# Block-sparse attention and a feed-forward on one core: P buffers, the order of weight conversion, and where adds run

## The chip, the cores and the metric

One core of one Trainium2 chip. The metric is the device time of one execution in microseconds. The kernel before has a median of 794.09 us in three runs (792.69 to 794.2).

## What is computed

Four batches, 8 heads of 64, 768 positions. Scores are q·kT/8; blocks of 32 keys that the pattern doesn't allow (window, first and last block, three sampled blocks a row) are set to -1e9; softmax; times v. The result, 768 x 512 a batch, goes through a normalized feed-forward with a residual. In the reference, cut:

```
attn = exp(scores - max); attn = attn / (sum(attn) + 1e-9); x = attn @ v
xn = (x - mean(x)) / sqrt(var(x) + 1e-6) * g_ln
out = x + maximum(xn @ w_ch1, 0) @ w_ch2        # w_ch1 512 x 2048, w_ch2 2048 x 512
```

The weights arrive as 64-bit floats, everything else as 32-bit.

## The kernel before, in words

**Tiling.** A *unit* is one batch's chunk of 256 queries: 12 units, three a batch. A unit has four *segments*, one a pair of heads, 48 in all; a segment has four *slots* (128 queries of one head). Two slots, the two heads for the same queries, are scored together: pair k holds slots 2k and 2k+1. Every fp32 operand of TensorE is split into two fp16 halves, high and low, and a product is three matmuls (high·high, low·high, high·low), except in the early segments.

**A slot's way.** `scores` (L591) into a PSUM tile `ps` (two of them); `masked_max` (L600, VectorE) writes the biased, negated scores to a tile P and their extreme to `st`; `exponent` (L614, ScalarE) turns P into exponentials. In the first nine segments (EARLY) TensorE transposes P in fp32 (L629) into one of three PSUM banks and ScalarE copies it out to `pt` (L636), and `weighted` (L714) multiplies by v in fp32. In later segments `attention` makes P's fp16 halves, high on ScalarE (L675), low on VectorE (L679), into places `ph` and `pl`, two each or, from segment WIDEAT on, four; SP transposes them by DMA (L685, L688), and `weighted` (L718, L723) follows. When a unit's four segments are done, `layer_norm` runs through VectorE, ScalarE and TensorE down to `xh` (L859) and `xl` (L863), and `ffn` does W1 then W2 (all in `product`, L306): 384 matmuls of 256 columns a unit.

**Weights.** W1 has 8 chunks (1,i), W2 16 chunks (2,i) of half the size. `loads_w` loads a chunk (L497, L507), and makes fp32 out of the 64-bit words in three steps on VectorE (L518, L522, L526). A chunk in PORC has a short third step instead (L531) and an add on GpSimd (L536). Then comes a scaling on ScalarE (L554) if the chunk is in neither PORC nor LOWDVE, the high half on ScalarE (L560, L562) or, if it is in both HIDMA and PORC, by a DMA (L572), and the low half: on VectorE (L568) if it is in LOWDVE, else on GpSimd (L566). Chunks of W2 from the third on are loaded when all of W1 is converted, those from the eleventh on when the first ten of W2 are.

**What sets the order.** All engines run an order that is written at build time. `Plan` is a list scheduler with a cost and a latency for every task; each engine takes, of the tasks that could start now, the one of lowest rank. Ranks are counted in slots: W1AT and W2AT for the chunks, KAT, VAT and QAT for loads, MASKAT for the second half of the mask, which slot 16 needs. Feed-forward matmuls have the last rank and fill what is left. EASE is the spare time that the planner leaves before a task that waits for another engine: its first value for ranks under EASY on TensorE, its second beyond, its third for other engines beyond EASY. A task with `lock` isn't started by the planner while GpSimd or VectorE holds one. Where TensorE would idle before KEEP (ns), the planner puts fillers (L298). AVHOLD = n: from segment 12 on, the weighted sum of segment i isn't issued before pair 2i+n. CASTK: the high half of K is cast on ScalarE (L362) for the first so many of the 16 K, by a DMA on GpSimd's queue after that; KDVE and QDVE: how many low halves of K (L355) and q (L391) VectorE makes, GpSimd the others.

**P's memory.** P is one of four rotating tiles; a slot takes one at its masked maximum and gives it back when its transposes (early) or its low half (later) are done. The places for the fp16 halves are tiles of their own.

Of the kernel before, what the change touches and what calls it, by code (L numbers as in the profile page):

```python
# [176 lines left out]
def sparse_attention_moe(  # L177
# [32 lines left out]
    EASY, EASE = 44, (249, 2530, 951)  # L210
    PORC = ((2, 0), (2, 7), (1, 1), (2, 11), (2, 9), (1, 6), (2, 13), (2, 10), (1, 4), (2, 1), (2, 2))
# [26 lines left out]
    pp = ctx.enter_context(tc.tile_pool(name="pp", bufs=2))  # L238
# [11 lines left out]

    plan = Plan()
# [92 lines left out]
    def loads_k(b, pr, rank, before):  # L344
        idx = b * NPAIR + pr
        o = SimpleNamespace()

        def raw():
# [3 lines left out]
            nc.sync.dma_start(o.kr, ks[b, pr])  # L352
# [4 lines left out]
        o.raw = plan.add("SP", 580, raw, (before,), rank, 2000, load=1120, order="k",  # L357
# [12 lines left out]
    def loads_q(n, rank, before):  # L370
        u, pr = segs[n].u, segs[n].pr
        o = SimpleNamespace()

        def raw():
# [62 lines left out]
    def loads_v(b, pr, rank, before):  # L437

        o = SimpleNamespace(idx=b * NPAIR + pr, vr={}, raw=[])
        early = any(x.early for x in segs if (x.u.b, x.pr) == (b, pr))  # L440
# [11 lines left out]
        for j in range(2):  # L452
            def raw(j=j):
# [18 lines left out]
    def loads_w(kind, i, before, w1done, low_tail):  # L472

        o = SimpleNamespace()
        own = (kind, i)
        if kind == 1:
# [11 lines left out]
        def load():  # L488
# [18 lines left out]
            nc.sync.dma_start(o.raw.rearrange("p e t -> p (e t)"),  # L507
# [33 lines left out]
        ld = plan.add("SP", 580, load, after if kind == 1 or i >= 10 else after + tuple(  # L541
# [52 lines left out]
    def masked_max(s):  # L594
        s.p = pp.tile([P, S], F32, tag="p", name=f"p{s.i}", bufs=4)
# [21 lines left out]
    def attention_early(seg, pair, e_done):  # L617
        r = pair[0].i
        for s in pair:
            key = (seg.i, s.h % 2)  # L620
            x4 = x2 = None
            for part, (lo, hi) in enumerate(((0, 4), (4, KT))):
# [18 lines left out]
                take = (("pt", key),) if s.t == 0 and part == 0 else ()  # L641
# [498 lines left out]
```

## Time and profile before

| | |
|---|---|
| median of three runs | 794.09 us |
| the profiled execution, its own time | 793.85 us |
| its span in the trace | 792.1 us |
| TensorE busy | 777.9 us |
| VectorE busy | 616.1 us |
| ScalarE busy | 507.2 us |
| GpSimd busy | 123.5 us |

The span runs from the first to the last instruction in the trace; the own time has in addition what lies around it. Durations in rows are of that one execution. In rows, PE is TensorE's matmuls, PEld its weight loads, DVE VectorE, ACT ScalarE, POOL GpSimd, SP the queue that issues most DMAs. Matmuls are pipelined and overlap in the rows: the distance from start to start is their cost. A wait for several semaphores is put down to the one that came last.

### The profile page before, as it was taken

What the parts mean: (1) busy time and instruction counts of PE and PEld (TensorE: products, weight loads), DVE (VectorE), ACT (ScalarE), POOL (GpSimd) and SP (SyncE); (2) the same over time, 40 slices, a digit from 0 to 9 for tenths busy, and PEclk for the clock granted to TensorE, in tenths of its full rate; (3) what the DMA queues carried; (4) which work ended last, traced back from release to release, by engine and by line L of the source; (5) the groups of instructions that cost most, each with busy time, mean ns of one, the idle gap of its engine ahead of it and who ended that gap; (6) DMA issues with size and microseconds to landing.
All of it is one profiled execution on the core that took longest, in us unless ns stands there. A gap on an engine that the chain in (4) does not pass through costs nothing.

```text
span 792.1 us, 18470 instructions
## 1 busy us (share of the span) xinstructions
PE 777.9 (98%) x7327; PEld 599.5 (76%) x7327; DVE 616.1 (78%) x1216; ACT 507.2 (64%) x946; POOL 123.5 (16%) x129
## 2 busy tenths in 40 slices
PE   8999999999999999999999999999999999999998
PEld 5656677778777777777777877777777777788887
DVE  6999999989878778989868677879978678854220
ACT  6789777676666567777756667687666657642110
POOL 1343542321101002312001001121010000000000
PEclk9999999999999999999999999999999999999999
DMA  9463436899967677999856557899865565741000
GB/s 320 169 191 124 143 107 156 184 208 150 177 116 138 126 127 151 196 166 174 146 119 132 114 118 147 158 200 160 158 144 126 109 138 110 122 108 27 21 1 27
DMA packets 285110, 109.07 MB, mean 138 GB/s; under 512 B 253792, under 2 KB 276832, under 8 KB 285024
## 3 DMA queue, kind: packets, MB, share of 16 engines
q1 hardware_dynamic: 278544, 104.91, 62.0%
q0 software_dynamic: 6192, 2.89, 3.2%
q8 instruction: 57, 0.93, 0.6%
q14 instruction: 29, 0.24, 0.1%
q10 hardware_dynamic: 288, 0.10, 0.1%
HBM read 42.84 MB, written 6.29 MB: 62 GB/s over the span
## 4 chain that ended last, share of the span: by engine, by line
PE 86%; DVE 6%; DMA 4%; ACT 3%; issue 1%; SPq 0%; ACTq 0%; DVEq 0%
PE bank L306 60%; PE ps L591 11%; PE pa L718 7%; PE pa L723 3%; PE pa L714 2%; PE bank L629 2%; DVE p L600 1%; DMA raw<-k 1%; DMA pt<-pl 1%; DMA w1r<-w 1%; ACT pt L636 1%; ACT p L614 1%; DVE pl L679 1%; DMA allow<-blocks 0%; PE pa L739 0%
## 5 line engine op out<-in xcount | busy, mean ns | idle before, releaser
L306 PE MATMUL bank<-hh,w2h 128*128 128x256 f16 x768 | 204.5, 273 | 0.0
L306 PE MATMUL bank<-hl,w2h 128*128 128x256 f16 x768 | 204.2, 273 | 0.0
L306 PE MATMUL bank<-hh,w2l 128*128 128x256 f16 x768 | 204.2, 273 | 0.0
L600 DVE CUSTOM_DVE_ANT_1 p<-ps,allow 128x768 f32<-128x768 f32 x192 | 177.9, 951 | 23.6 <-PE ps L591 23.0
L614 ACT ACTIVATE p<-p,st 128x768 f32<-128x768 f32 x192 | 178.3, 930 | 22.7 <-DVE st L600 22.6
L306 PEld LDWEIGHTS <-w1h 128*128 128x128 f16 x1536 | 147.6, 98 | 27.4 <-issue 10.6
L306 PEld LDWEIGHTS <-w2h 128*128 128x128 f16 x1536 | 147.2, 98 | 25.6 <-issue 8.9
L306 PE MATMUL bank<-xh,w1h 128*128 128x256 f16 x768 | 115.4, 273 | 1.5 <-ACT pt L636 1.0
L306 PE MATMUL bank<-xl,w1h 128*128 128x256 f16 x768 | 115.3, 273 | 1.0 <-DVE xl L863 1.0
L306 PE MATMUL bank<-xh,w1l 128*128 128x256 f16 x768 | 115.4, 273 | 0.0
L902 DVE SCALAR_TENSOR_TENSOR hl<-bank,hh 128x512 f16<-128x512 f32 x96 | 66.1, 689 | 52.3 <-ACT hh L896 51.4
L896 ACT ACTIVATE hh<-bank 128x512 f16<-128x512 f32 x96 | 56.8, 592 | 76.6 <-PE bank L306 76.1
L675 ACT ACTIVATE ph<-p,st 128x768 f16<-128x768 f32 x88 | 78.7, 926 | 29.8 <-issue 15.3
L679 DVE SCALAR_TENSOR_TENSOR pl<-p,st,ph 128x768 f16<-128x768 f32 x88 | 88.8, 1026 | 1.9 <-ACT hh L896 0.9
L306 PEld LDWEIGHTS <-w1l 128*128 128x128 f16 x768 | 73.7, 98 | 12.7 <-issue 4.3
L306 PEld LDWEIGHTS <-w2l 128*128 128x128 f16 x768 | 75.0, 98 | 9.1 <-issue 0.3
L718 PE MATMUL pa<-pt,vh 128*64 128x512 f16 x468 | 80.0, 383 | 0.4 <-DMA pt<-pl 0.3
L675 ACT ACTIVATE raw<-p,st 128x768 f16<-128x768 f32 x68 | 60.8, 927 | 19.2 <-issue 10.1
L679 DVE SCALAR_TENSOR_TENSOR raw<-p,st,raw 128x768 f16<-128x768 f32 x68 | 72.6, 1086 | 0.1
L388 POOL DMA_DIRECT2D qh<-q x42 | 24.3, 578 | 284.3 <-PE ps L591 249.7
L591 PE MATMUL ps<-kh,qh 64*128 64x256 f16 (+1 forms) x384 | 66.0, 328 | 1.5 <-DVE st L600 1.4
L591 PE MATMUL ps<-kl,qh 64*128 64x256 f16 (+1 forms) x384 | 64.3, 323 | 1.4 <-DVE kl L355 1.4
(111 smaller groups left out, 982.7 us busy)
## 6 DMA issues: line engine op xcount, KB each, us to landing
qr<-q SPq DMA_DIRECT2D x48, 128.0 KB, 2.8
raw<-k SPq DMA_DIRECT2D x16, 384.0 KB, 4.1
raw<-w SPq DMA_DIRECT2D x12, 512.0 KB, 3.9
vr<-v SPq DMA_DIRECT2D x32, 192.0 KB, 3.0
out<-ot SPq DMA_DIRECT2D x48, 128.0 KB, 1.9
w2l<-w SPq DMA_DIRECT2D x4, 1024.0 KB, 8.2
qh<-q POOLq DMA_DIRECT2D x42, 64.0 KB, 2.8
pt<-raw SPq DMA_TRANSPOSE x136, 2.7
```

The lines of the kernel that those rows point to most:

```text
L306: nc.tensor.matmul(dst, w, x, start=start, stop=stop, skip_group_check=True)
L388: o.high = plan.add("POOL", 560, lambda: nc.gpsimd.dma_start(o.qh, qs[u.b, pr, u.c]), (o.raw,), rank, 2300, load=400, order="q")
L591: nc.tensor.matmul(s.ps[:, lo:hi], x[rows, s.qs], y[rows, lo:hi], start=n == 0, stop=n == len(terms) - 1)
L600: nc.vector.tensor_tensor_reduce(out=s.p.rearrange(blk, k=BLK), in0=s.ps[:, 0:S].rearrange(blk, k=BLK), in1=bias, scale=-0.125, scalar=3.0 ...
L614: nc.scalar.activation(s.p, s.p, AF.Exp, bias=s.st[:, j : j + 1], scale=-1.0, accum_out=total)
L629: nc.tensor.transpose(dst[:, (t - lo) * P : (t - lo + 1) * P], s.p[:, t * P : (t + 1) * P], ident)
L675: nc.scalar.activation(s.ph, s.p, AF.Copy, scale=s.r)
L679: nc.vector.scalar_tensor_tensor(out=s.pl, in0=s.p, scalar=s.r, in1=s.ph, op0=ALU.mult, op1=ALU.subtract)
L718: nc.tensor.matmul(seg.pa[half[hh], 0 : 2 * CH], vo.vh[:, hh, t, :], pts[keys[hh]][:, t].rearrange("p i n -> p (i n)"), start=t == 0, stop ...
L723: nc.tensor.matmul(seg.pa[half[hh], 0:CH], vo.vl[:, hh, t, :], pts[keys[hh]][:, t, 0, :], start=False, stop=t == KT - 1, skip_group_check= ...
L896: nc.scalar.activation(u.hh[:, f : f + 2, :].rearrange("p f n -> p (f n)"), bank[plan.where("bank", own)], AF.Relu)
L902: nc.vector.scalar_tensor_tensor(out=u.hl[:, f : f + 2, :].rearrange("p f n -> p (f n)"), in0=bank[plan.where("bank", own)], scalar=0.0, i ...
```

## The change

Two tiles more for P in the first seven segments: the memory of the fp16 halves is bound as a fifth and sixth P, and segment 9, the first that writes halves, waits for the transposes of those early slots (`wides`). P is no longer taken in rotation but as the place that comes free first. (1,3) joins PORC, which has twelve chunks now; in LOWDVE (2,3) is replaced by (1,5). All W2 ranks lie below 21.01. WIDEAT, AVHOLD, CASTK, QDVE, MASKAT, the two slacks' limit EASY and the other ranks change, and so do some of the planner's costs. `queue_of` could move loads to another queue, but POOLQ is empty.

```diff
-    EASY, EASE = 44, (249, 2530, 951)
-    PORC = ((2, 0), (2, 7), (1, 1), (2, 11), (2, 9), (1, 6), (2, 13), (2, 10), (1, 4), (2, 1), (2, 2))
+    EASY, EASE = 38, (222, 2530, 951)
+    PORC = ((2, 0), (2, 7), (1, 1), (2, 11), (2, 9), (1, 6), (2, 13), (2, 10), (1, 4), (2, 1), (2, 2), (1, 3))
-    SPLITAT = 7.38
+    SPLITAT = 6.58
-    KDVE, QDVE = 3, 1
-    HIDMA = ((1, 5), (2, 15), (2, 2), (1, 7), (2, 5), (2, 4))
-    LEAD = 2.8
-    HIGHAT, LOWAT = -0.42, -1.36
-    EVAC, EXPO = -9.12, 1.22
-    WIDEAT = 14
-    PLAIN = 'full'
-    LOWDVE = ((2, 12), (1, 3), (2, 2), (1, 6), (1, 1), (2, 8), (2, 11), (1, 7), (2, 4), (2, 15), (2, 6), (2, 3), (1, 0), (2, 13), (2, 5))
-    AVHOLD = 4
-    KEEP = 40000.0
-    CASTK, CASTQ = 16, 6
-    MASKAT = 25.07
-    KAT, VAT, QAT = 11.39, 7.48, 12.65
-    AVAT = -17.05
-    W1AT = (8.87, 9.4, 10.72, 12.06, 12.3, 15.45, 16.92, 18.19)
-    W2AT = (10.6, 14.04, 14.21, 15.7, 17.12, 20.44, 21.31, 22.16, 23.71, 24.25, 25.32, 25.67, 25.7, 25.75, 26.19, 28.74)
+    KDVE, QDVE = 3, 2
+    HIDMA = ((1, 5), (2, 2), (1, 7), (2, 5), (2, 4), (1, 2))
+    LEAD = 1.32
+    POOLQ = ()
+    WIDEAT = 18
+    HIGHAT, LOWAT = -0.28, -0.16
+    EVAC, EXPO = -13.82, 1.9
+    PLAIN = 'cols'
+    LOWDVE = ((2, 12), (1, 3), (2, 2), (1, 6), (1, 1), (2, 8), (2, 11), (1, 7), (2, 4), (2, 15), (2, 6), (1, 0), (2, 13), (2, 5), (1, 5))
+    AVHOLD = 5
+    KEEP = 60000.0
+    CASTK, CASTQ = 12, 6
+    MASKAT = 28.03
+    KAT, VAT, QAT = 7.07, 12.75, 10.68
+    AVAT = -17.65
+    W1AT = (8.99, 9.42, 10.08, 11.38, 11.61, 14.48, 16.19, 16.46)
+    W2AT = (11.84, 14.42, 16.13, 16.55, 18.07, 18.39, 19.14, 19.35, 19.7, 19.93, 19.99, 20.2, 20.39, 20.68, 20.71, 21.0)
...
+    plan.choice("p", range(6))
...
+    p_s = [const.tile([P, S], F32, name=f"p{i}") for i in range(4)]
+    halves_s = [const.tile([P, 2, S], F16, name=f"p{n}") for n in "hl"]
+    p_s += [x.rearrange("p i s -> p (i s)").bitcast(F32) for x in halves_s]
...
-        s.p = pp.tile([P, S], F32, tag="p", name=f"p{s.i}", bufs=4)
+        s.p = p_s[plan.where("p", s.i)]
...
+                if part and seg.i < EARLY - 2:
+                    wides.append(x)
...
-            h = plan.add("ACT", 830, high, (inv,) + done, r, 120, take=(("ph", s.i, 2, places),))
-            l = plan.add("DVE", 930, low, (h,) + done, r, 100, lock=True, take=(("pl", s.i, 1, places),),
+            free = tuple(wides) if seg.i == EARLY else ()
+            h = plan.add("ACT", 830, high, (inv,) + free + done, r, 120, take=(("ph", s.i, 2, places),))
+            l = plan.add("DVE", 930, low, (h,) + free, r, 100, lock=True, take=(("pl", s.i, 1, places),),
...
-            th = plan.add("SP", 1310, turn_high, (h,), r, 1500, load=1250, give=(("ph", s.i),),
+            th = plan.add("SP", 1310, turn_high, (h,), r, 1600, load=1150, give=(("ph", s.i),),
...
-                                  s.i, 160, take=(("p", s.i),), give=(("ps", s.i),), order="m")
+                                  s.i, 160, give=(("ps", s.i),), order="m",
+                                  take=(("p", s.i, 1, range(6 if seg.i < EARLY - 2 else 4)),))
```

## Rows read from the trace of the kernel before

**Rows 1.** The page's first part: busy time of each engine, its share of the span, and its instructions.
```profile
PE 777.9 (98%) x7327; PEld 599.5 (76%) x7327; DVE 616.1 (78%) x1216; ACT 507.2 (64%) x946; POOL 123.5 (16%) x129
```
**Rows 2.** Busy time in stretches of the span: the stretch and its length, busy us (and instructions) of PE, PEld, DVE, ACT and POOL, the granted clock, the busy share of the DMA engines, GB/s.
```profile
0.00:90.00 90.00, 81.15 (x681) 54.46 (x683) 80.93 (x145) 73.69 (x158) 35.12 (x34) 1.00 0.57 191
90.00:165.00 75.00, 74.06 (x686) 57.09 (x684) 70.13 (x147) 51.25 (x100) 23.28 (x21) 1.00 0.67 156
165.00:785.00 620.00, 619.04 (x5936) 484.87 (x5932) 464.64 (x925) 382.22 (x688) 65.08 (x75) 1.00 0.68 129
```
**Rows 3.** The fillers, from the groups of instructions on TensorE: count, busy us and mean ns, idle us before them.
```profile
L298 PE MATMUL bank<-ones,ones_h 128*128 128x256 f16 x67 | 9.8, 309 | 1.2 <-DVE eps L275 1.2
```
**Rows 4.** TensorE's timeline, the first scores: start us, us from there to the end of the last of them.
```profile
5.83 0.39 PE L591 MATMUL ps<-kh,qh 64*128 64x512 f16 x2
```
**Rows 5.** Busy time in two more stretches, with the columns of rows 2.
```profile
30.00:60.00 30.00, 27.22 (x238) 17.23 (x236) 28.76 (x47) 25.84 (x55) 11.90 (x10) 1.00 0.45 138
60.00:90.00 30.00, 28.00 (x236) 19.37 (x238) 28.36 (x53) 26.30 (x60) 15.32 (x13) 1.00 0.36 116
```
**Rows 6.** Who waited for whom from 0 to 90 us, rows of TensorE and its weight loads: us in total, times, longest.
```profile
PEld bank L629 <- ACT pt L636: 6.8, 16, 1.1
...
PEld bank L629 <- ACT p L614: 2.3, 6, 0.8
...
PE ps L591 <- DVE st L600: 1.4, 3, 0.6
```
**Rows 7.** Timelines of TensorE and VectorE around unit 3's start: pair 34, the first and last matmuls of segment 15's weighted sum and what follows, pair 35, xl of unit 3, its first W1 matmuls.
```profile
244.90 0.39 PE L591 MATMUL ps<-kh,qh 64*128 64x512 f16 x2
...
245.97 0.41 PE L718 MATMUL pa<-pt,vh 128*64 128x512 f16 x2
...
248.05 0.28 PE L306 MATMUL bank<-hh,w2h 128*128 128x256 f16 x1
...
252.08 0.39 PE L591 MATMUL ps<-kh,qh 64*128 64x512 f16 x2
...
272.36 1.22 DVE L863 TENSOR_TENSOR xl<-xc,xh 128x1024 f16<-128x1024 f32 x1
...
273.12 0.60 PE L306 MATMUL bank<-xh,w1h 128*128 128x256 f16 x4
```
**Rows 8.** Timelines of ScalarE and TensorE around unit 7's start; the idle time before an instruction and what ended it stand in brackets.
```profile
514.34 0.83 ACT L362 CAST kh<-raw 128x768 f16<-128x768 f32 x1 [2.87 <-DMA raw<-k]
...
519.05 0.60 PE L306 MATMUL bank<-xl,w1h 128*128 128x256 f16 x4 [0.96 <-DVE xl L863]
```
**Rows 9.** Groups of instructions by line and shape over the span: a full and a short third step of W1, low halves of W1 on VectorE, scalings of W1 on ScalarE. Count, busy us and mean ns, idle us before them.
```profile
L526 DVE SCALAR_TENSOR_TENSOR w2h<-w2h 128x1024 int32<-128x1024 int32 x1 | 1.2, 1211 | 0.0
...
L531 DVE TENSOR_SCALAR w2h<-w2h 128x1024 int32<-128x1024 int32 x1 | 0.7, 670 | 0.0
...
L568 DVE SCALAR_TENSOR_TENSOR w1l<-w2h,w1h 128x1024 f16<-128x1024 f32 x5 | 6.3, 1259 | 0.2 <-ACT w1h L562 0.2
...
L554 ACT ACTIVATE w2h<-w2h 128x1024 f32<-128x1024 f32 x2 | 2.1, 1063 | 0.0
```
**Rows 10.** Timelines of ScalarE and TensorE: a scaling of W1, and the transposes that waited for a copy behind it.
```profile
59.38 1.06 ACT L554 ACTIVATE w2h<-w2h 128x1024 f32<-128x1024 f32 x1
...
60.75 1.14 PE L629 MATMUL bank<-ident,p 128*128 128x128 f32 x6 [0.89 <-ACT pt L636]
```
**Rows 11.** Timelines of VectorE and GpSimd where they ran side by side: part of the second mask and a W1 add; a third step and a low half.
```profile
24.62 3.29 DVE L321 TENSOR_TENSOR allow<-allow,w1h 128x96 f32<-128x96 f32 x3
...
25.09 2.41 POOL L536 TENSOR_TENSOR w2h<-w2h,w1r 128x1024 int32<-128x1024 int32 x1
...
56.30 2.43 DVE L526 SCALAR_TENSOR_TENSOR w2h<-w2l,w2h 128x1024 int32<-128x1024 int32 x1
...
55.52 2.13 POOL L566 TENSOR_TENSOR w1l<-w2h,w1h 128x1024 f16<-128x1024 f32 x1 [1.15 <-ACT w1h L560]
```
**Rows 12.** Timelines: the transposes of slot 15 on TensorE and the masked maximum of slot 19 on VectorE (slots by counting L629 and L600).
```profile
51.53 0.87 PE L629 MATMUL bank<-ident,p 128*128 128x128 f32 x6
...
52.52 0.95 DVE L600 CUSTOM_DVE_ANT_1 p<-ps,allow 128x768 f32<-128x768 f32 x1
```
**Rows 13.** TensorE's timeline: fillers, and the scores of pair 5 behind them.
```profile
27.38 1.69 PE L298 MATMUL bank<-ones,ones_h 128*128 128x256 f16 x14
29.68 0.37 PE L591 MATMUL ps<-kh,qh 64*128 64x512 f16 x1 [0.60 <-DVE st L600]
```
**Rows 14.** Groups of instructions on VectorE from 126.6 to 153.3 us, two of the five that belong to W2.
```profile
L568 DVE SCALAR_TENSOR_TENSOR w2l<-raw,w2h 128x512 f16<-128x512 f32 x4 | 2.7, 685 | 0.4 <-ACT w2h L562 0.4
L522 DVE SCALAR_TENSOR_TENSOR raw<-raw 128x512 int32<-128x512 int32 x4 | 2.7, 684 | 0.0
```
**Rows 15.** TensorE's timeline: the first scores of pairs 20 and 24.
```profile
127.33 0.39 PE L591 MATMUL ps<-kh,qh 64*128 64x512 f16 x2
...
169.06 0.39 PE L591 MATMUL ps<-kh,qh 64*128 64x512 f16 x2
```
**Rows 16.** The chain that ended last, two pairs of scores that follow each other in it: start us, us.
```profile
199.31 1.08 PE ps L591 x12
...
206.06 1.08 PE ps L591 x12
```
**Rows 17.** Issues of DMAs, the transposes of the low halves of P: count, KB each if known, median us from issue to landing.
```profile
pt<-pl SPq DMA_TRANSPOSE x88, 2.8
```

More of the change, by code (lines that the diff above doesn't have):

```diff
@@ L249, in sparse_attention_moe, with queue_of @@
     ctx.enter_context(tc.manual_schedule(engines={ET.SP, ET.Pool, ET.DVE, ET.Activation}))
+    def queue_of(kind):
+        return (nc.gpsimd, "POOL", 900) if kind in POOLQ else (nc.sync, "SP", 580)
     plan = Plan()
@@ L254, in sparse_attention_moe @@
     plan.mode, plan.plain = None, PLAIN
-    for name, size in (("k", 4), ("v", 4), ("vr", 2), ("q", NQ), ("qr", 3), ("ps", 2), ("p", 4),
+    for name, size in (("k", 4), ("v", 4), ("vr", 2), ("q", NQ), ("qr", 3), ("ps", 2),
                        ("pt", 5), ("pa", 1), ("xT", 3), ("xh", 1),
@@ L346, in loads_k @@
         o = SimpleNamespace()
+        qk = "k" if b else ""
         def raw():
@@ L351, in raw @@
             o.kr = raw_s[RAWS.index(plan.where("raw", ("k", idx)))][:, 0:S]
-            nc.sync.dma_start(o.kr, ks[b, pr])
+            queue_of(qk)[0].dma_start(o.kr, ks[b, pr])
         def low():
             (nc.vector if idx < KDVE else nc.gpsimd).tensor_sub(o.kl, o.kr, o.kh)
-        o.raw = plan.add("SP", 580, raw, (before,), rank, 2000, load=1120, order="k",
+        o.raw = plan.add(*queue_of(qk)[1:], raw, (before,), rank, 2000, load=1120, order="k",
                          take=(("k", idx), ("raw", ("k", idx), 2 if idx < RAWS_S else 1, RAWS)))
@@ L364, in loads_k @@
             o.high = plan.add("POOL", 560, lambda: nc.gpsimd.dma_start(o.kh, ks[b, pr]),
-                              (o.raw,), rank, 2300, load=1100, order="k")
+                              (o.raw,), rank, 2300, load=1500, order="k")
         e, x = ("DVE", 870) if idx < KDVE else ("POOL", 1640)
@@ L372, in loads_q @@
         o = SimpleNamespace()
+        qk = "q" if n >= 8 else ""
         def raw():
@@ L378, in raw @@
                 o.ql = ql_s[plan.where("q", n)]
-            nc.sync.dma_start(o.qr, qs[u.b, pr, u.c])
-        o.raw = plan.add("SP", 580, raw, (before,), rank, 2000, load=370, order="q",
+            queue_of(qk)[0].dma_start(o.qr, qs[u.b, pr, u.c])
+        o.raw = plan.add(*queue_of(qk)[1:], raw, (before,), rank, 2000, load=370, order="q",
                          take=(("q", n), ("qr", n)) if n >= RAWS_S else (("qr", n),))
@@ L388, in loads_q @@
             o.high = plan.add("POOL", 560, lambda: nc.gpsimd.dma_start(o.qh, qs[u.b, pr, u.c]),
-                              (o.raw,), rank, 2300, load=400, order="q")
+                              (o.raw,), rank, 2300, load=600, order="q")
         e, x = ("DVE", 345) if n < QDVE else ("POOL", 660)
@@ L439, in loads_v @@
         o = SimpleNamespace(idx=b * NPAIR + pr, vr={}, raw=[])
+        qv = "v" if b else ""
         early = any(x.early for x in segs if (x.u.b, x.pr) == (b, pr))
@@ L459, in raw @@
                     dst = o.vr[j] = rawp.tile([P, KT, D], F32, tag="vr", name=f"vr{o.idx}_{j}")
-                nc.sync.dma_start(dst.rearrange("p t d -> p (t d)"), v[b, 2 * pr + j])
+                queue_of(qv)[0].dma_start(dst.rearrange("p t d -> p (t d)"), v[b, 2 * pr + j])
             take = (() if early else (("vr", (o.idx, j)),)) + ((("v", o.idx),) if j == 0 else ())
-            o.last = plan.add("SP", 580, raw, (o.last,), rank, 2000, load=550, take=take, order="v")
+            o.last = plan.add(*queue_of(qv)[1:], raw, (o.last,), rank, 2000, load=550, take=take, order="v")
             o.raw.append(o.last)
@@ L475, in loads_w @@
         own = (kind, i)
+        qw = "w" if kind == 2 else ""
         if kind == 1:
@@ L540, in loads_w @@
             after += tuple(low_tail)
-        ld = plan.add("SP", 580, load, after if kind == 1 or i >= 10 else after + tuple(
+        ld = plan.add(*queue_of(qw)[1:], load, after if kind == 1 or i >= 10 else after + tuple(
             w1done if not low_tail and i > 1 else ()), rank - LEAD, 2000,
@@ L572, in loads_w @@
             o.high = plan.add("POOL", 560, lambda: nc.gpsimd.dma_start(o.dh, o.src), (d,), rank + HIGHAT,
-                              2300, load=1500 * size)
+                              4300, load=2270 * size)
         else:
```

12 lines of the change are left out of this document (5 added, 7 removed).

## The prediction, made before the change was run

> **What bounds the kernel now.** I read the page first: TensorE is busy for 98% of the span, VectorE and ScalarE for 78% and 64% [rows 1]. Busy time on TensorE is modelled and says little by itself, so I cut the span into stretches [rows 2]. The granted clock is 1.00 in each. From 165 to 785 us TensorE idles 0.96 of 620 us, and from 90 to 165 us 0.94 of 75. Nothing that shortens another engine there can shorten the run; it can only spoil it. From 0 to 90 us TensorE is busy 81.15 us, and 9.8 of these are fillers that compute nothing [rows 3], so 90 - 81.15 + 9.8 = 18.65 us do no useful work. The first scores start at 5.83 us [rows 4], after the first loads, which the change leaves alone. That leaves 18.65 - 5.83 = 12.8 us as all that can come back early.
>
> Who is late there? From 30 to 90 us VectorE is busy 57.1 of 60 us and ScalarE 52.1 [rows 5]. TensorE's transposes wait for ScalarE's copies out of PSUM, 6.8 us in 16 waits; 2.3 us are waits for exponentials and 1.4 for masked maxima [rows 6]. So ScalarE comes last most often, with VectorE close behind; both are nearly saturated, and a new order gives something only where it fills one of their holes.
>
> There is a second place. Each unit's feed-forward needs its normalized input, and units 3 and 7 get it at the last moment: unit 3's first matmul is at 273.12 us while xl is still being made (272.36 + 1.22 = 273.58) [rows 7], and at unit 7 TensorE waits 0.96 us for xl [rows 8]. An attention stage that comes later than now costs time there, although TensorE looks full.
>
> **The change, part by part.** The sum is made against the profiled execution: span 792.1 us, its own time 793.85, which is 0.24 under the median of 794.09.
>
> *Conversions.* Chunk (1,5) enters LOWDVE: ScalarE loses one scaling of 1.06 us, GpSimd a low half, VectorE gains a low half of 1.26 [rows 9]. The scaling at 59.38 stands right ahead of the copies for which TensorE then waits 0.89 us at 60.75 [rows 10]. I take -0.9; ends 0 (VectorE becomes late instead) and -1.06. Chunk (1,3) enters PORC: VectorE's third step falls from 1.21 to the short form, of which the fastest took 0.67 [rows 9], say 0.4 less, and GpSimd gets an add of 2.41 [rows 11]. Chunk (2,3), half the size, leaves LOWDVE: VectorE loses about half of 1.26, ScalarE gains about half of 1.06. The low half of segment 1's q goes from GpSimd to VectorE: 256 columns, a quarter of 1.26. VectorE's balance is 1.26 - 0.4 - 0.6 + 0.3 = +0.6, ScalarE's -0.5, in 90 us: nothing, with -0.5 and +0.6 as ends.
>
> The adds have a hidden price. VectorE's L526 at 56.30 took 2.43 us, against 1.21 elsewhere, while GpSimd's L566 ran from 55.52 to 57.65; three small L321 took 3.29 together around the GpSimd add at 25.09 [rows 9, 11]. A meeting of this kind cost 2.43 - 1.21 = 1.2 us. The planner's lock keeps the two engines apart in its own times, so I take 0 for the twelfth add, with +1.2 as the end. The Trainium skill ("SBUF — State Buffer", section "Who interferes with whom") says that a VectorE instruction with two SBUF inputs and a GpSimd instruction that reads SBUF lock each other out, whichever starts second waiting for the whole of the other. This trace agrees, with the stretched L526. By that rule alone the add would meet one such instruction and the result would be 792.3 us.
>
> *Six P buffers.* With four, slot 19's masked maximum (52.52) came 0.12 us after the transposes of slot 15 let go of its P (51.53 + 0.87) [rows 12]. With six, VectorE and ScalarE may run one pair of slots further ahead of TensorE. What this can save is TensorE's waits for exponentials and maxima, 2.3 + 1.4 = 3.7 us at most [rows 6]; at least nothing, as ScalarE's copies stay. I take -1.5, nearer the small end because the copies end most waits.
>
> *The second mask.* It was built around 24.62 to 28 us, ahead of slot 8's masked maximum, and TensorE issued 14 fillers from 27.38 until the scores behind that maximum at 29.68, 2.3 us [rows 11, 13]. A later MASKAT and more P give VectorE other work there, but slot 16 still needs the mask. I take -0.7; ends 0 and -2.3.
>
> *All W2 ahead.* From 126.6 to 153.3 us VectorE still spends 2.7 + 2.7 us on just two of the steps of W2 [rows 14], and pairs 20 to 24 of scores need from 127.33 to 169.06, 10.4 us a pair [rows 15], where later pairs stand 6.75 to 7.2 apart [rows 7, 16]. The change takes this work out of there, but puts it ahead of slots 17 to 24, so the pairs in between come later. What stays as a gain is only VectorE's idle time that gets filled: 75 - 70.13 = 4.9 us from 90 to 165 [rows 2]. I take pair 24 to be 3 us earlier; ends 0 and 5. Each chunk's load moves with it through SP's queue, where the DMA engines were 0.36 busy from 60 to 90 us [rows 5]. TensorE is full meanwhile, so this is worth nothing directly; its worth is at units 3 and 7.
>
> *AVHOLD 4 to 5.* The weighted sum of segment 15 starts at 245.97, right behind pair 34 (244.90); now it waits for pair 35 (252.08) [rows 7]. Behind it are unit 3's normalization and its whole feed-forward. The added wait is 252.08 - 244.90 = 7.2 us, less the pull of 3 above: 4.2, plus the 0.46 by which xl was already late. In the gap TensorE can run the displaced weighted sum (2.1 us, 245.97 to 248.05) and a pair of scores (1.1) [rows 7]: 4.7 - 3.2 = +1.5. Ends 0 (pair 24 earlier by more) and +7.7. At unit 7 this delay is already in the feed-forward, and what stalled it goes: ScalarE waited 2.87 us for a K load before its cast, with xh behind it [rows 8]. The casts of the last four K become DMAs on GpSimd's queue, which is busy 65 of 620 us from 165 on [rows 2]; they stand there in front of q loads that are needed several pairs later. That is -1.0; ends -1.0 and 0.
>
> *At nothing:* HIDMA (only (2,2) is in both lists, before and after), PLAIN (no task asks for mode "any"), SPLITAT, POOLQ. Two places instead of four for P's halves in segments 14 to 17 hold while a pair lasts 6.75 us and a transpose lands in 2.8 [rows 16, 17]; else up to +1. The other ranks and slacks reorder two saturated engines: -2 to +3, and I take 0.
>
> Sum: -0.9 - 1.5 - 0.7 + 1.5 - 1.0 = -2.6, so 793.85 - 2.6 = 791.2 us.
>
> **Rivals.** *The hold decides* (slower). If pair 24 does not start before some 165 us, segment 15's weighted sum is a whole pair late, unit 3 starts 7.7 late, and nothing later gives it back, since TensorE has no idle time after it; the gains of the first 90 us (3.1) stay: 793.85 + 7.7 - 3.1 = 798.4. For it: the hold binds, with the weighted sum 1.07 us behind its pair's first scores [rows 7]. Against it: VectorE is free of W2 sooner. *The early holes close* (faster). If half of the 12.8 us goes and the attention is a full pair ahead at unit 3: 793.85 - 6.4 - 1.0 = 786.4. For it: the holes are many small ones; against it: ScalarE's load there falls by only half a microsecond. *Nothing moves.* Both engines are saturated, their sums unchanged, the holes change place: 793.9. For it [rows 5]; against it, that a whole order is replaced. A last one (slower): W2 ahead of attention starves TensorE before unit 0's feed-forward, when only attention feeds it. One chunk of some 2 us ahead of each of slots 20 to 23 is +8, less the 3.1: 798.8.
>
> **How the numbers follow.** Forecast 0.35; early holes 0.19; nothing 0.17; the hold 0.24; starving 0.05. Faster is 0.35 + 0.19 = 0.54; same, which is within 0.2% or 1.6 us, about what a measurement of this kernel can tell from no change, 0.17; slower 0.24 + 0.05 = 0.29. The forecast's own range is 788 to 793.5, from its ends. The whole range reaches past both outer cases by about a microsecond or two: 784.5 to 799.5.
>
> **What would show it.** Right: fewer fillers and at least 2.5 us more useful TensorE time in 0 to 90 us; the last W2 low half well before 130 us; pair 24 at 164 to 167 us; the weighted sum of segment 15 behind pair 35, with unit 3 starting within 2 us of unit 2's end; no K cast ahead of xh at unit 7. Wrong: TensorE idle by several us at the start of unit 3 or 4; or useful time in 0 to 90 us unchanged; or VectorE instructions of twice their length beside GpSimd's in that stretch.

## The result, and the profile after

The kernel after takes 798.71 us (median; 796.38 to 801.66), the kernel before 792.96 beside it: a ratio of 1.0077, interval 1.0064 to 1.0089. It is **slower by some 6 us** (5.8 between these medians, 6.1 by the ratio), where 2.6 less was forecast; the range held it, the direction was wrong. The profiled execution of after took 801.05 us (span 799.2), 2.3 above its median, and that of before 793.85. The two traces are 7.1 us of span apart. Its mean granted clock over the span, 0.991, is the lowest that the eight executions had (0.991 to 1.00), so this trace shows more of the half clock than the median has.

The stretches of [rows 2 and 5], now of after:
```profile
0.00:90.00 90.00, 77.99 (x598) 52.20 (x600) 78.13 (x132) 65.67 (x138) 28.90 (x28) 0.92 0.54 182
30.00:60.00 30.00, 24.77 (x183) 15.25 (x183) 26.86 (x42) 21.72 (x44) 11.55 (x10) 0.88 0.45 140
60.00:90.00 30.00, 27.28 (x209) 19.21 (x209) 27.15 (x45) 22.65 (x50) 9.96 (x8) 0.90 0.29 92
90.00:165.00 75.00, 73.27 (x686) 55.44 (x683) 71.11 (x145) 55.80 (x113) 26.90 (x25) 1.00 0.66 148
165.00:785.00 620.00, 620.00 (x5953) 485.56 (x5951) 475.30 (x939) 383.23 (x694) 68.33 (x80) 1.00 0.68 132
```
Read the counts behind TensorE's time: by 90 us it has begun 598 matmuls, against 681 [rows 2]. From 90 to 165 us both begin 686. From 165 to 785 us after begins 17 more. A matmul of that last stretch takes 620/5953 = 0.104 us, so 83 - 17 = 66 of them are 6.9 us, close to the 7.1 between the spans. By this count **all of the loss arises in the first 90 us**, nothing is lost at the hand-over between units, and a little is won later. VectorE and ScalarE are not busier there but idler than before, and the granted clock is 0.92 instead of 1.00. The three stretches of half clock (0.50, the 1.2 GHz level):
```profile
32.06:35.47 3.41, 3.41 (x14) 1.64 (x16) 3.08 (x4) 2.04 (x5) 1.18 (x3) 0.50 0.16 22
55.96:62.79 6.83, 6.47 (x30) 3.63 (x31) 6.67 (x10) 5.58 (x11) 2.71 (x2) 0.50 0.87 315
79.85:83.26 3.41, 3.38 (x18) 2.29 (x18) 3.41 (x7) 2.67 (x8) 0.00 (x0) 0.50 0.78 306
```
What TensorE waited for from 0 to 90 us (us in total, times, longest); in before the first of these stood at 1.4 us in 3 waits, the second at 6.8 in 16 [rows 6]:
```profile
PE ps L602 <- DVE st L611: 7.2, 7, 2.0
PEld bank L640 <- ACT pt L647: 4.9, 10, 1.2
```
Scores now wait for masked maxima. VectorE's timeline ahead of the longest of these waits:
```profile
47.95 2.64 DVE L533 SCALAR_TENSOR_TENSOR w2h<-w2h 128x1024 int32<-128x1024 int32 x1
...
51.71 3.38 DVE L579 SCALAR_TENSOR_TENSOR w1l<-w2h,w1h 128x1024 f16<-128x1024 f32 x1
55.01 0.94 DVE L611 CUSTOM_DVE_ANT_1 ph<-ps,allow 128x768 f32<-128x768 f32 x1
...
55.89 0.95 DVE L611 CUSTOM_DVE_ANT_1 pl<-ps,allow 128x768 f32<-128x768 f32 x1
```
and GpSimd's beside it (L547 is a W1 add, the first of the two the new one of chunk (1,3), the second that of (1,4); L400 is a low half of q):
```profile
46.44 2.42 POOL L547 TENSOR_TENSOR w2h<-w2h,w2l 128x1024 int32<-128x1024 int32 x1
48.81 0.68 POOL L400 TENSOR_TENSOR ql<-qr,qh 128x256 f16<-128x256 f32 x1
51.60 2.40 POOL L547 TENSOR_TENSOR w2h<-w2h 128x1024 int32<-128x1024 int32 x1 [2.12 <-DVE w2h L542]
```
Such instructions take 1.21 to 1.26 us elsewhere [rows 9]. Here L579 starts 0.11 us after an add, and ends at 55.09, which is 1.09 us after the add's end at 54.00: it did its work once GpSimd had finished. L533 ends 1.1 us after L400. These two meetings cost 1.43 + 2.17 = 3.6 us (less 1.21 each), and the masked maxima of slots 16 and 17 stand right behind. In before GpSimd's add at that place was the following, and what it met was the masked maxima of slots 18 and 19, whose lengths stayed 0.96 and 0.95 us (the second in [rows 12]):
```profile
51.30 2.40 POOL L536 TENSOR_TENSOR w2h<-w2h 128x1024 int32<-128x1024 int32 x1 [4.13 <-DVE w2h L531]
```
```profile
51.63 0.96 DVE L600 CUSTOM_DVE_ANT_1 p<-ps,allow 128x768 f32<-128x768 f32 x1 [0.15 <-PE ps L591]
```
TensorE's side in after:
```profile
53.38 0.60 PE L809 MATMUL bank<-xT,ones 128*128 128x256 f32 x2
56.02 0.58 PE L602 MATMUL ps<-kh,qh 64*128 64x512 f16 x1 [2.04 <-DVE st L611]
...
58.91 1.54 PE L640 MATMUL bank<-ident,ph 128*128 128x128 f32 x6
```
It was idle for 2.04 us, the clock was at half as it resumed, and six transposes take 1.54 us where [rows 12] have 0.87. So a 3.6 us delay on VectorE becomes an idle TensorE, and that a slow one.

### The profile page after: what moved, and what is told of

Same layout as the page of the kernel before. It is cut to its first block, busy times and chain, and to the rows that moved or that the text cites. A ratio compares the mean times of both kernels' runs of the same rounds, so it can differ in the third digit from the quotient of the medians.

```text
span 799.2 us, 18445 instructions
## 1 busy us (share of the span) xinstructions
PE 782.1 (98%) x7328; PEld 602.7 (75%) x7328; DVE 625.8 (78%) x1217; ACT 504.7 (63%) x942; POOL 124.1 (16%) x133
## 4 chain that ended last, share of the span: by engine, by line
PE 91%; DVE 6%; DMA 1%; issue 0%; ACT 0%; ACTq 0%; SPq 0%; DVEq 0%
PE bank L313 64%; PE ps L602 12%; PE pa L732 7%; PE pa L737 3%; PE pa L728 2%; PE bank L640 2%; DVE p L611 1%; DVE w2h L533 1%; DMA w1r<-w 1%; DVE allow L328 0%; DVE w2h L537 0%; DVE w1l L579 0%; DVE pl L611 0%; PE pa L753 0%; DVE w2h L529 0%
## 5 line engine op out<-in xcount | busy, mean ns | idle before, releaser
L611 DVE CUSTOM_DVE_ANT_1 p<-ps,allow 128x768 f32<-128x768 f32 x184 | 170.4, 951 | 22.6 <-PE ps L602 22.5
L625 ACT ACTIVATE p<-p,st 128x768 f32<-128x768 f32 x184 | 170.5, 929 | 16.8 <-DVE st L611 16.8
L688 ACT ACTIVATE ph<-p,st 128x768 f16<-128x768 f32 x96 | 86.1, 928 | 35.9 <-issue 16.3
L692 DVE SCALAR_TENSOR_TENSOR pl<-p,st,ph 128x768 f16<-128x768 f32 x96 | 99.3, 1045 | 3.6 <-DMA pt<-pl 2.5
L602 PE MATMUL ps<-kh,qh 64*128 64x256 f16 (+1 forms) x384 | 68.1, 331 | 7.2 <-DVE st L611 7.2
L602 PEld LDWEIGHTS <-qh 64*128 64x128 f16 x768 | 31.5, 95 | 52.2 <-issue 29.8
L602 PE MATMUL ps<-kl,qh 64*128 64x256 f16 (+1 forms) x384 | 66.4, 327 | 0.6 <-DVE kl L363 0.6
L602 PE MATMUL ps<-kh,ql 64*128 64x256 f16 (+1 forms) x384 | 65.6, 327 | 0.0
L400 POOL TENSOR_TENSOR ql<-qr,qh 128x256 f16<-128x256 f32 x46 | 39.7, 862 | 166.0 <-DMA qr<-q 118.3
```

The costliest lines, as they stand in the source:

```text
L400: o.low = plan.add(e, x, lambda: (nc.vector if n < QDVE else nc.gpsimd).tensor_sub(o.ql, o.qr, o.qh), (o.raw, o.high), rank, give=(("qr", ...
L602: nc.tensor.matmul(s.ps[:, lo:hi], x[rows, s.qs], y[rows, lo:hi], start=n == 0, stop=n == len(terms) - 1)
L611: nc.vector.tensor_tensor_reduce(out=s.p.rearrange(blk, k=BLK), in0=s.ps[:, 0:S].rearrange(blk, k=BLK), in1=bias, scale=-0.125, scalar=3.0 ...
L625: nc.scalar.activation(s.p, s.p, AF.Exp, bias=s.st[:, j : j + 1], scale=-1.0, accum_out=total)
L688: nc.scalar.activation(s.ph, s.p, AF.Copy, scale=s.r)
L692: nc.vector.scalar_tensor_tensor(out=s.pl, in0=s.p, scalar=s.r, in1=s.ph, op0=ALU.mult, op1=ALU.subtract)
```

## The experiments

The last column counts the matmuls that TensorE had begun by 90 us without fillers: x of the window 0 to 90 less x of the fillers' group, as 598 - 68 = 530 for after and 681 - 67 = 614 for before. It is of one execution, the profiled one: in those of e6 and e7 the mean clock was 0.91 in the first 20 us, and TensorE began 113 and 111 matmuls there, against 131 in after and e1. Ratios are to before on the same chip.

| run | edit | ratio | interval | useful matmuls by 90 us |
|---|---|---|---|---|
| after | none | 1.0077 | 1.0064 to 1.0089 | 530 |
| e6 | after less the add of (1,3) | 1.0033 | 1.0021 to 1.0045 | 560 |
| e1 | after less four W1 adds | 0.9985 | 0.9976 to 0.9993 | 596 |
| e7 | memsets for the four adds | 0.9994 | 0.9986 to 1.0003 | 586 |
| e5 | before less its three W1 adds | 0.9970 | 0.9959 to 0.9981 | 626 |
| e2 | after, more fillers | 1.0039 | 1.0027 to 1.0051 | 553 |
| e3 | after, W ranks of before | 1.0069 | 1.0054 to 1.0085 | 520 |
| e4 | after, AVHOLD 4 | 1.0054 | 1.0039 to 1.0068 | 566 |
| e8 | after, both lists of before | 1.0035 | 1.0023 to 1.0048 | 600 |
| e11 | e1 with four P | 0.9991 | 0.9982 to 1.0000 | 596 |
| e12 | e1 with AVHOLD 4 | 0.9985 | 0.9977 to 0.9994 | 596 |
| e9 | after, no W1 on GpSimd | 1.0140 | 1.0118 to 1.0161 | 498 |
| e10 | before, no W1 on GpSimd | 1.0075 | 1.0053 to 1.0098 | 548 |
| e13 | after, adds in pieces | 1.0035 | 1.0023 to 1.0047 | 576 |
| e14 | before, adds in pieces | 0.9996 | 0.9984 to 1.0007 | 616 |
| e15 | after, adds and lows in pieces | 1.0063 | 1.0040 to 1.0086 | 532 |
| e16 | before, adds and lows in pieces | 1.0000 | 0.9992 to 1.0009 | 612 |
| e17 | before, last K by DMA | 0.9993 | 0.9985 to 1.0002 | 618 |
| e18 | e14 and e17 together | 0.9994 | 0.9985 to 1.0003 | 610 |

**The four W1 adds, out (e1).**
```
         def third_add():
-            nc.gpsimd.tensor_tensor(out=o.wf, ..., op=ALU.add)
+            kind == 1 or nc.gpsimd.tensor_tensor(out=o.wf, ..., op=ALU.add)
```


> The changed kernel with GpSimd's four adds on W1 chunks left out (the chunks lack their scale and low bits; the order on VectorE, ScalarE, TensorE and SyncE is the same). In the changed kernel's trace three VectorE instructions next to these adds are longer by 2.1, 1.4 and 2.2 us (at 24.66, 47.95 and 51.71). Collision theory: these go, the scores that TensorE waited for at 56 us come 2 us or more earlier, and its granted clock falls less often: 3 to 6 us less than the changed kernel (798.7), so 793 to 796. Order theory (too much conversion ahead of attention starves TensorE in any case): under 1.5 us less, 797 to 799. Hold theory (AVHOLD): no change, 798 to 799.

792.83 us, which by the two ratios is 7.3 us below after: more than the 3 to 6 of the collision theory, and far from the other two. The wait of scores for masked maxima fell from 7.2 to
```profile
PE ps L602 <- DVE st L611: 2.8, 4, 1.3
```
The hold and the order cannot be what costs these 7.3 us, since both were left in. What the adds do not explain stands later, in stretches of e1 with the columns of [rows 2]:
```profile
30.00:60.00 30.00, 27.01 (x236) 17.49 (x233) 27.27 (x45) 25.52 (x53) 9.51 (x9) 1.00 0.51 161
60.00:90.00 30.00, 26.48 (x215) 20.00 (x213) 28.97 (x51) 24.31 (x54) 9.90 (x11) 0.94 0.34 100
```
From 30 to 60 us e1 is level with before (236 matmuls against 238, clock 1.00); from 60 to 90 it is not (215 against 236, clock 0.94). So the third stretch of half clock is not shown to be the adds' doing. In after pair 12 waits there, at 78.30, for a masked maximum that stands behind three W1 instructions of 1.22 us each (73.89, 75.02 and 76.16), none beside an add:
```profile
78.30 0.37 PE L602 MATMUL ps<-kh,qh 64*128 64x512 f16 x1 [1.27 <-DVE st L611]
```
In e8, with before's lists, the clock is 1.00 from 60 to 90 us. Which edit makes this wait was not tried by itself.

**More fillers (e2)**: 10, 18 and 16 ahead of the scores of pairs 5, 9 and 12.
```
 class Plan:
+    MORE = {10: 10, 18: 18, 24: 16}
...
-            t.emit()
+            self.more(t); t.emit()
```
`more` puts the fillers ahead of the scores of the slots that MORE names.

> The changed kernel with 10, 18 and 16 more fillers on TensorE ahead of the scores of pairs 5, 9 and 12, where it idles for 1.9, 2.3 and 2.5 us; nothing else is moved. Clock theory: the three stretches at half clock (3.4, 6.8 and 3.4 us) shrink or go and 1.5 to 4 us come back: 794.5 to 797. If the clock only falls where TensorE has nothing late to do, the clock comes back and the time does not: 798 to 799. If the fillers are longer than the pauses they cost up to 1 us.

```profile
0.00:90.00 90.00, 80.58 (x665) 55.74 (x666) 80.38 (x137) 68.32 (x143) 30.42 (x30) 1.00 0.57 189
```
The clock stays at 1.00 and 3.0 us come back, though 44 matmuls that compute nothing were added (0.31 us for one in [rows 3]). So the half clock, over all three stretches, is some 3 of the 6 us (by the intervals, 2 to 4), and 1.0039 is what is left at full clock. After's own executions agree: 796.38 and 798.03 us at a granted clock of 1.00, 801.05 and 801.66 at 0.991.

**The ranks of W (e3) and the hold (e4).**
```
-    W1AT = (8.99, 9.42, ...); W2AT = (11.84, 14.42, ...)
+    W1AT = (8.87, 9.4, ...); W2AT = (10.6, 14.04, ...)
```
```
-    AVHOLD = 5
+    AVHOLD = 4
```


> The changed kernel with the ranks W1AT and W2AT of the kernel before (planned anew). Order theory: most of the loss goes, 792 to 795. Collision theory: a new order meets GpSimd elsewhere, so anything between 793 and 800, told by the sum of stretched VectorE instructions in 30 to 60 us (4.6 us in the changed kernel, 2.4 before). Hold theory: 798 or more, as AVHOLD is still 5.

> The changed kernel with AVHOLD 4. Its trace has TensorE busy for all of 620 us from 165 on and unit 3 starting 1 us after its input, so the hold costs nothing by it: within 1 us of 798.7 and the first 165 us as they were. Hold theory (my prediction's rival): 4 to 7 us less, 792 to 795.

e3 stands at 1.0069 with the same stretched instructions (2.63 and 3.39 us): the ranks are not it. e4 stands at 1.0054; its interval overlaps that of after. In its profile L533 and L579 take 2.64 and 3.38 us again, and scores wait 7.6 us for maxima, but the clock stays at 1.00 and that execution took 796.68 us: the same meetings are not followed by half clock each time. Without the adds (e12, below) no worth of the hold is seen.

**Which add, and what before's adds cost (e5, e6).** The edit of e1, for all W1 chunks of before, and for (1,3) alone in after (`own == (1, 3) or ...`).

> The kernel before, with GpSimd's three W1 adds of that kernel left out (chunks (1,1), (1,6), (1,4) lack their low bits); every other instruction stays where it is. It says how much such adds cost where the schedule has only three of them. Leaving out four took 7.3 us from the kernel after. Theory A (a chain: the adds of after stretch VectorE's instructions at places where masked maxima are due right behind, late maxima stop TensorE, its clock falls): before has the maxima clear of it, lost only 27.1 us by 90 us against 35.3, so little is to be had here, 791 to 793.5. Theory B (each GpSimd add on the way of a W1 chunk costs about the same anywhere, 7.3/4 = 1.8 us): 787 to 789.

> The kernel after with only the new add, that of chunk (1,3), left out (that chunk lacks its low bits); the other three W1 adds stay, and all orders. Theory A with the new add as the trigger: 3.6 us of stretching of VectorE's instructions at 44 to 54 us loses its 1.42 us part directly and most of what follows, the late maxima at 55 and the half clock behind them: 794 to 796. Theory B (each add has an equal part of the 7.3 us): 796.5 to 797.5. Theory C (the new add is hidden, and the other moves cost the time): 798 to 799.

The new add alone is worth 0.44% (3.5 us), with no overlap of the intervals, and the three that both kernels have are worth 0.48% in after against 0.30% (2.4 us) in before. The 796.38 us of e6 lies between the ranges of theories A and B, but 3.5 is about half of 7.3, not a quarter. In e6 the low half of (1,3), L579, is done before (1,4)'s add starts at 54.11, and keeps its length; what meets that add is L529, the first step of a chunk, with 1.77 us instead of 0.7:
```profile
52.39 1.21 DVE L579 SCALAR_TENSOR_TENSOR w1l<-w2h,w1h 128x1024 f16<-128x1024 f32 x1
...
55.28 1.77 DVE L529 TENSOR_SCALAR w2h<-w2l 128x1024 int32<-128x1024 int32 x1
```
Of the 6.1 us between the kernels, the W1 adds carry 7.3 - 2.4 = 4.9 us. Theory B, an equal price for each add, falls: its 787 to 789 for e5 was 791.59.

**Latency or collision (e7).** Taking an add away also takes GpSimd out of the chain from VectorE to ScalarE. The memsets leave it in.
```
-            nc.gpsimd.tensor_tensor(out=o.wf, in0=o.wf, in1=o.raw[:, :, 0], op=ALU.add)
+            (nc.gpsimd.tensor_tensor(...) if kind == 2 else [nc.gpsimd.memset(x, 0.0) for x in (
+                o.raw[:, :, 0].bitcast(F32), o.raw[:, :, 0].bitcast(F32), o.wf[:, 0:1].bitcast(F32))])
```


> The kernel after with each of the four W1 adds replaced by three GpSimd memsets, two of the chunk's low words and one of the first column of its result (so W1 lacks low bits and one column of each of the four chunks is zero): GpSimd is still in the chain between VectorE and ScalarE and takes a similar time, but reads nothing from SBUF. Theory A (VectorE's instructions are stretched beside GpSimd's add): if the memsets leave them at their own length, 793 to 795; where the trace shows them stretched beside memsets too, 797 to 799. Theory D (the add's latency in the chunk's chain, GpSimd between VectorE and ScalarE, is what costs): 797 to 799 with VectorE's instructions at their own length.

GpSimd, then VectorE beside it:
```profile
44.80 2.21 POOL L547 MEMSET w2l<- 128x1024 f32 x2
...
49.09 2.18 POOL L547 MEMSET w2h<- 128x1024 f32 x3 [0.98 <-DVE w2h L542]
```
```profile
46.36 1.21 DVE L533 SCALAR_TENSOR_TENSOR w2h<-w2h 128x1024 int32<-128x1024 int32 x1
...
50.06 1.21 DVE L579 SCALAR_TENSOR_TENSOR w1l<-w2h,w1h 128x1024 f16<-128x1024 f32 x1
```
GpSimd is about as long in the chain (2.2 us against 2.4), L533 and L579 run beside it at their own length, and the time is 793.04. So the meetings with the adds cost 0.83%, and the latency some 0.09%, with the intervals of e1 and e7 overlapping. The Trainium skill ("SBUF — State Buffer", section "Who interferes with whom") says that a VectorE instruction with two SBUF inputs contends with a GpSimd instruction that reads SBUF, not with one that only writes it. These rows agree: 3.38 us beside the add, 1.21 beside memsets.

**Both lists of before (e8).**
```
-    PORC = (..., (1, 3)); LOWDVE = (..., (2, 6), (1, 0), ..., (1, 5))
+    PORC = (...); LOWDVE = (..., (2, 6), (2, 3), (1, 0), ...)
```


> The kernel after with the two lists of the kernel before (which W chunks end as GpSimd adds, which are finished by VectorE): eleven adds, three of them W1's; (1,3) is whole on VectorE again, (1,5) ends on ScalarE and GpSimd. The planner places everything anew. Theory A with the new add as trigger: 793.5 to 796, and a trace with under 3.5 us of stretched excess on VectorE in 30 to 60. Theory C (the other edits cost the time: six P, mask, hold, order): 797.5 to 799.

By 90 us TensorE has begun 600 useful matmuls, against 530 in after and 614 in before: with the lists put back, most of the early loss is gone. But the time, 796.95 us, lies between the ranges of both theories. The new order loses time at another place (5911 matmuls from 165 to 785 us, against 5936 in before), where a weighted sum waits for the transposes of P and the clock falls again. Window and timeline of e8:
```profile
160.00:200.00 40.00, 37.95 (x346) 29.81 (x345) 33.09 (x65) 27.60 (x48) 8.46 (x9) 0.96 0.88 170
```
```profile
167.01 0.38 PE L732 MATMUL pa<-pt,vh 128*64 128x512 f16 x1 [1.45 <-DMA pt<-pl]
167.99 0.38 PE L732 MATMUL pa<-pt,vh 128*64 128x512 f16 x1 [0.60 <-DMA pt<-pl]
```

**Six P and the hold, with no adds in the way (e11, e12).**
```
-                 take=(("p", s.i, 1, range(6 if seg.i < EARLY - 2 else 4)),)
+                 take=(("p", s.i, 1, range(4)),)
...
-            free = tuple(wides) if seg.i == EARLY else ()
+            free = ()
```


> The kernel after without its four W1 adds (those chunks lack their low bits) and with four places for P throughout instead of six early: what six places are worth where no collision hides it; beside it stands the same kernel with six, 792.8. The prediction's term of -1.5 us for six P: 794 to 795. P's places bind nowhere: 792 to 793.5. The early transposes from more places collide with more: under 792.

> The kernel after without its four W1 adds (those chunks lack their low bits) and with the weighted sums held back by 4 again instead of 5; beside it stands the same kernel with 5, 792.8. The prediction's term of +1.5 us for the hold: 791 to 792. The hold costs nothing, since the attention is far enough ahead: 792.4 to 793.5.

0.9991 and 0.9985 beside 0.9985: neither is told apart from nothing.

**Can the adds be avoided (e9, e10)?** `PORC` without its W1 chunks, so that VectorE ends them.

> The kernel after with all four W1 chunks taken from the list of GpSimd adds, so that VectorE ends them in one instruction (2.4 us of GpSimd's latency and the collisions go; VectorE pays some 0.5 us more for each of the four). The computation is whole; the planner places everything anew. Theory A (collisions): 7.3 us less 2.1 us of VectorE's work, if all of that shows, 793 to 795.5. Theory B2 (VectorE is the bound there, the adds were worth their collisions): 797 to 800. If the rest of the change is worth something by itself, 790 to 792.

> The kernel before with its three W1 chunks taken from the list of GpSimd adds: the same edit on the other kernel. Leaving its adds out was worth 0.3% (2.4 us); VectorE pays 1.6 us more. Theory A: 791.5 to 794. Theory B2 (VectorE is the bound): 794.5 to 797.

Both kernels get slower: after by another 0.6%, before by 0.75%. I had put this at 2.1 and 1.6 us of VectorE's time at most, and both times lie above every range that I gave. TensorE has begun 498 and 548 useful matmuls by 90 us, so the loss is early again. The planner made a new order for both, so VectorE's added work and the new places are not separated, and which of them costs the time stays open. What it does show is that in these orders GpSimd's adds are worth more than their meetings cost.

**Short pieces (e13 to e16).**
```
-            nc.gpsimd.tensor_tensor(out=o.wf, in0=o.wf, in1=o.raw[:, :, 0], op=ALU.add)
+            [nc.gpsimd.tensor_tensor(out=o.wf[:, x], in0=o.wf[:, x], in1=o.raw[:, x, 0], op=ALU.add)
+             for x in (slice(j, j + 256) for j in range(0, 1024 if kind == 1 else 512, 256))]
```
e15 and e16 cut the low halves (`nc.gpsimd.tensor_sub`) in the same way.

> The kernel after, whole, with each GpSimd add cut into instructions of 256 columns (four for a W1 chunk, two for a W2 chunk), in the same places of all orders. In the traces a stretched VectorE instruction ended about its own 1.2 us after the GpSimd instruction beside it had ended, as if it had waited for all of it. If so (theory E: one waits for the other's whole instruction), a VectorE instruction now waits for at most one piece, some 0.7 us instead of up to 2.2: 794 to 797. If both run at a lower rate side by side (theory F), pieces change nothing but GpSimd's own overhead: 798.5 to 800.

> The same edit on the kernel before. Its W1 adds were worth 2.4 us in all. Theory E: 791.5 to 793.5. Theory F: 793.5 to 795.

> The kernel after, whole, with GpSimd's adds and its low halves of the W chunks cut into instructions of 256 columns. The low halves stretch VectorE's instructions by 1.05 and 1.08 us at 44 and 60.6 us. Theory E: another 1 to 2 us below the run with the adds alone, 793 to 796. Theory F: 798.5 to 801.

> The same edit on the kernel before. Theory E: 791 to 793. Theory F: 794 to 796.

e13 gives back 0.42% with the work whole. VectorE in e13, then GpSimd:
```profile
45.96 3.04 DVE L533 SCALAR_TENSOR_TENSOR w2h<-w2h 128x1024 int32<-128x1024 int32 x1
...
50.12 1.72 DVE L579 SCALAR_TENSOR_TENSOR w1l<-w2h,w1h 128x1024 f16<-128x1024 f32 x1
```
```profile
44.46 2.82 POOL L547 TENSOR_TENSOR w2h<-w2h,w2l 128x256 int32<-128x256 int32 x4
47.24 0.66 POOL L400 TENSOR_TENSOR ql<-qr,qh 128x256 f16<-128x256 f32 x1
50.01 3.80 POOL L547 TENSOR_TENSOR w2h<-w2h 128x256 int32<-128x256 int32 x4 [2.10 <-DVE w2h L542]
```
At 50.12 VectorE gets in after one piece and GpSimd is the one that waits (four pieces take 3.80 us instead of 2.82): theory E. At 45.96 it does not: L533 starts during the pieces and ends 1.1 us after the q low half behind them, so it got in neither between the pieces nor ahead of that low half. Short pieces help where VectorE gets its turn, and here it got it in one of two meetings. e15 shows the second kind at its worst, VectorE and then GpSimd:
```profile
45.18 4.49 DVE L529 TENSOR_SCALAR w2h<-w2h 128x1024 int32<-128x1024 int32 x1 [1.20 <-POOL w1l L577]
```
```profile
45.68 2.81 POOL L547 TENSOR_TENSOR w2h<-w2h,w2l 128x256 int32<-128x256 int32 x4
48.46 0.66 POOL L400 TENSOR_TENSOR ql<-qr,qh 128x256 f16<-128x256 f32 x1
```
An instruction of 0.7 us took 4.49, through five of GpSimd's, and it reads one operand from SBUF, not two. It starts 0.09 us after a DMA issue of GpSimd's (L397, 45.09, 0.57 us) and ends 0.55 after the fifth. e15 is not below e13, and its 798.64 us falls in the range of theory F; its rows still look like theory E, one engine waiting for the other's whole instructions, only for a row of them. In before pieces show no gain (0.9996, 1.0000), though e5 has 0.30% there; e14 and e16 do not tell E from F.

**The step on unit 7 by itself (e17, e18).**
```
-    CASTK, CASTQ = 16, 6
+    CASTK, CASTQ = 12, 6
```


> The kernel before, whole, with one edit of the change alone: the last four K are cast by DMA (CASTK 12 instead of 16). All orders are those of before until unit 5's feed-forward. The prediction's term for it: -1.0 us, since ScalarE's 2.87 us wait ahead of unit 7's xh goes; 792.4 to 793 where before has 793.5, ratio 0.9985 to 0.9995. If that wait is made good elsewhere: 1.000. Beside it, in the trace, TensorE's time lost between 500 and 600 us should fall from 3.7 to 2.6 us, as it did in after.

> The same, and GpSimd's adds in pieces of 256 columns: the two edits that may help the kernel before, together. Pieces alone stood at 0.9996 of before. If both terms add up: 0.998 to 0.999, 792 to 792.7. If neither is real: 1.000.

TensorE's window around unit 7's start in e17; in before it was busy 99.04 of these 100 us:
```profile
500.00:600.00 100.00, 100.00 (x963) 77.47 (x961) 82.46 (x165) 66.49 (x123) 14.96 (x18) 1.00 0.90 160
```
The hole closes, as after's does. The time, 0.9993 and 0.9994, is not told apart from no change: no whole version here is shown to be below before.

## Why the prediction was wrong

**The step that failed** is the price of the twelfth add: "The planner's lock keeps the two engines apart in its own times, so I take 0 for the twelfth add, with +1.2 as the end." The new add alone measured 3.5 us (e6), the four together 7.3 (e1), where before's three cost 2.4 (e5). By e1 and e5 the rest of the change is worth about +1.2 us (their intervals overlap), where the sum had -2.6. Three things were left out of the add's price:

- The lock holds in the planner's times, and the chip is not on them. [rows 11] already showed a stretched L526 in before, under the same lock: the evidence that the lock fails stood beside the sentence that relied on it.
- One meeting was priced at 1.2 us. L579 lost 2.17, because it starts right behind an add's start and waits for all of it. That add is not even the new one: with an add of its own, chunk (1,3) has its low half at 51.71, beside (1,4)'s add, where in before the low half stood at 46.82 (below) and (1,4)'s add met masked maxima, which are not stretched.
- A delay on VectorE was priced as itself. It was late for the masked maxima, TensorE idled 2.04 us, and the clock fell; e2 puts the clock's part, over all three stretches, at some 3 us. No rival had the clock in it, since it was 1.00 in every row of before [rows 2].

```profile
46.82 1.44 DVE L568 SCALAR_TENSOR_TENSOR w1l<-w2h,w1h 128x1024 f16<-128x1024 f32 x1
```

By the Trainium skill's rule alone the prediction made 792.3 us, still faster than before (its own sum gives 791.2 + 1.2 = 792.4). The rule agrees with the rows above. What fell short was one meeting at 1.2 us: there were two here, of 1.43 and 2.17 us, and TensorE waited behind them.

**The other terms.** *Six P*, -1.5: e11, with four, stands 0.06% (some 0.5 us) above e1, and the intervals overlap: not told apart from 0. *The second mask*, -0.7: it did not move off the add. In after it stands beside one again, with the 3.29 us that [rows 11] show:
```profile
24.01 3.29 DVE L328 TENSOR_TENSOR allow<-allow,w1h 128x96 f32<-128x96 f32 x3
```
*Conversions*, -0.9 for chunk (1,5): not tried by itself; e8 undoes it with the rest of the lists and is faster, not slower. *All W2 ahead*: the step did not take place as I read it. The last low half of W2 on VectorE starts at 159.45 (I had said well before 130), and e3 says that the ranks move nothing. Pair 24 is at 174.90, 5.84 behind [rows 15], with TensorE 83 matmuls (8.6 us at 0.104) behind by then: some 2.8 earlier by that count, against the 3 that I took. What that is worth was not tried by itself.
```profile
159.45 0.69 DVE L579 SCALAR_TENSOR_TENSOR w2l<-raw,w2h 128x512 f16<-128x512 f32 x1
```
```profile
174.90 0.39 PE L602 MATMUL ps<-kh,qh 64*128 64x512 f16 x2
```
*AVHOLD*, +1.5: the weighted sum of segment 15 does stand behind pair 35, but xl of unit 3 is done at 284.88, ahead of the 286.04 at which it is wanted. No cost is seen (e12), my lower end. Pair 35, the weighted sum, xl, unit 3's W1:
```profile
253.91 0.39 PE L602 MATMUL ps<-kh,qh 64*128 64x512 f16 x2
...
254.98 0.41 PE L732 MATMUL pa<-pt,vh 128*64 128x512 f16 x2
...
286.04 0.50 PE L313 MATMUL bank<-xh,w1h 128*128 128x256 f16 x3
```
```profile
283.67 1.21 DVE L877 TENSOR_TENSOR xl<-xc,xh 128x1024 f16<-128x1024 f32 x1
```
*Unit 7's K cast*, -1.0: right in mechanism and in TensorE's time (620.00 of 620 against 619.04; e17), too small to be seen in the whole.

**The rivals.** The hold named 798.4 and starving 798.8, both close to what came, and both for a cause that the runs exclude: the hold by e4 and e12, W2's order by e1 and e3. Starving had the right place, TensorE fed by attention alone ahead of unit 0's feed-forward, but what starves it up to 60 us is VectorE's waiting for GpSimd, not W2's order. The wait at 78.30, behind W1 instructions, is of its kind, and small. The mark that decides stood last in the list of what would be wrong: "VectorE instructions of twice their length beside GpSimd's in that stretch."

**What stays open.** Without adds after is at 0.9985 and before at 0.9970; the intervals overlap, so that 0.15% is not shown to be there. If it is, the stretch from 60 to 90 us of e1 is where to look. Why e9 and e10 lose so much is not separated.

## What to carry to other kernels

Before moving work to GpSimd, list which VectorE instructions will run beside it: price each meeting at GpSimd's remaining run, and then look at what is queued behind the stretched instruction. A lock in a planner's times is no lock on the chip, and one stretched instruction in the trace of before shows that. Where TensorE has no other work, price an idle gap of 2 us also with what the clock may do after it.

## What the runs showed of the hardware that was not expected

- VectorE can wait for a whole row of GpSimd instructions: 4.49 us for an instruction of 0.70 (e15), 3.04 for one of 1.21 (e13); in another meeting of e13 it got in between two pieces (1.72). What decides is not shown.
- GpSimd's memsets left the same VectorE instructions at 1.21 us (e7). Masked maxima, which read PSUM and SBUF, stayed at 0.96 and 0.95 beside before's add at 51.30.
- 44 added fillers made a kernel faster by 0.38%, with the granted clock at 1.00 to 90 us instead of 0.92 (e2).
